# Moving the first loads of k, v and q into one GpSimd DMA row with the first weight matrix

## The chip, the cores and the metric

The kernel runs on one core of a Trainium2 chip. The metric is the device time of one execution in microseconds (us); the time of a run is about 1.8 us longer than the span of its trace. A single core has no second die to compare with, so I checked the granted TensorE clock of each run instead (the share of its full clock that TensorE was allowed): 0.99 to 1.0 in all but one kernel, which is told as such.

## The reference

For each of 8 batches and 8 heads (576 positions, head size 64) a linear attention: features of q and k are the positive part times a cosine and times a sine of the position, concatenated. Then one dense layer with a squared ReLU.

```python
k_p, q_p = phi(k), phi(q)                  # (B, H, S, 128)
kv  = einsum('bhsf,bhsd->bhfd', k_p, v);  z = k_p.sum(axis=2)
x   = einsum('bhsf,bhfd->bhsd', q_p, kv) / (einsum('bhsf,bhf->bhs', q_p, z) + 1e-6)
x   = x.transpose(0, 2, 1, 3).reshape(4608, 512)
out = maximum(x @ w_in, 0)**2 @ w_out      # w_in 512 x 2048, w_out 2048 x 512
```

## The kernel before

Positions of a batch are split in a main part (512, four blocks of 128) and a tail (64). `load` fetches one of q, k, v for a batch: one transfer of 1 MB (two halves for the first q), then two of 64 KB for the tail.

```python
def load(src, nm, b, eng, parts=1):
    main = inp.tile([P, H, J, D], F32, ...); tail = inp.tile([P, HH, D], F32, ...)
    for i in range(parts):
        eng.dma_start(out=main[:, :, js, :], in_=src[b, :, 0:MAIN, :]...)    # rows of 1 KB (512 B in halves)
    for g in range(2):
        eng.dma_start(out=tail[g*TAIL:(g+1)*TAIL], in_=src[b, ..., MAIN:S, :]...)   # rows of 256 B
```

`load_w1` fetches a quarter of w_in from the GpSimd queue and converts it to bf16 on the way (1 MB read, 512 KB written). The start of the program, which is all that the change touches:

```python
load_batch(0, nc.sync, "kv")
load(q, "q", 0, nc.sync, 2)
constants()                       # position constants, identity: GpSimd, ScalarE
warm(34)                          # filler products that keep TensorE running
for j in range(NS): att_k(0, j)   # features of k on VectorE (cos) and ScalarE (sin)
att_v(0, J - 1, nc.gpsimd, H - 1, H)   # GpSimd copies one head of v ...
att_v(0, 0, nc.vector); att_v(0, 1, nc.scalar); att_v(0, 2, nc.vector)
att_v(0, 3, nc.vector, 0, H - 1)       # ... VectorE the other seven of that block
att_v(0, J, nc.vector)                 # v's tail
for i in range(4): load_w1(i, 4)       # w_in, behind GpSimd's copy
load_batch(1, nc.gpsimd, "q"); load_w2(0, 4)   # [...] later loads, same queue
att_kv(0, 0); att_kv(0, 1)             # "kz": k features times v
att_feat(0, 0); att_feat(0, 1)         # features of q
# [...] transposes of q ("tq"), "num", division, transposes of x, then the w_in products ("hps")
```

The engines run their instructions in order (an experiment below shows VectorE held up for 2.21 us by this). Each DMA issue on GpSimd waits for the landing of the one eight issues back (in the profile of before the tenth issue, a tail of batch 1's k, waits 2.48 us, until the second quarter of w_in has landed). The w_in products of batch 0 come in eight groups; the first four each need a new quarter of w_in.

Of the kernel before, what the change touches and what calls it, by code (L numbers as in the profile page):

```python
# [19 lines left out]
def kernel(  # L20
# [9 lines left out]
    nc = tc.nc  # L30
    P = nc.NUM_PARTITIONS
    B, H, S, D = q.shape
# [6 lines left out]
    J = S // P  # L39
# [18 lines left out]

    kqv = {}

    def load(src, nm, b, eng, parts=1):
        main = inp.tile([P, H, J, D], F32, name=nm, tag=nm, bufs=2)
        tail = inp.tile([P, HH, D], F32, name=nm + "t", tag=nm + "t", bufs=2)
        for i in range(parts):
            js = slice(i * J // parts, (i + 1) * J // parts)
            eng.dma_start(
                out=main[:, :, js, :],
                in_=src[b, :, 0:MAIN, :].rearrange("h (p j) d -> p h j d", j=J)[:, :, js, :],
            )
        for g in range(2):  # L70
            eng.dma_start(
                out=tail[g * TAIL : (g + 1) * TAIL, :, :],
                in_=src[b, g * HH : (g + 1) * HH, MAIN:S, :].rearrange("h p d -> p h d"),
            )
        kqv[nm, b] = (main, tail)

    def load_batch(b, eng, order):
        for nm in order:
            load({"k": k, "v": v, "q": q}[nm], nm, b, eng)

    def piece(nm, b, j):
        main, tail = kqv[nm, b]
        return main[:, :, j, :] if j < J else tail[:, :, :]
# [8 lines left out]
    def constants():  # L92
        sidx = const.tile([P, J + 1], F32, name="sidx")
        for p0, p1, c, n, base, mult in [
            (0, P, 0, J, 0, J),
            (0, TAIL, J, 1, MAIN, 1),
            (TAIL, P, J, 1, MAIN, 1),
        ]:
            nc.gpsimd.iota(
                sidx[p0:p1, c : c + n],  # L100
                pattern=[[1, n]],
                base=base,
                channel_multiplier=mult,
                allow_small_or_imprecise_dtypes=True,
            )
        bias_pi2 = const.tile([P, 1], F32, name="bias_pi2")
        nc.vector.memset(bias_pi2, math.pi / 2.0)
        theta_scale = (math.pi / 2.0) / S
        nc.scalar.activation(cos_col, sidx, ACTF.Sin, bias=bias_pi2[:], scale=-theta_scale)
        nc.scalar.activation(sin_col, sidx, ACTF.Sin, bias=0.0, scale=theta_scale)  # L110
        make_identity(nc, ident)
# [5 lines left out]
    def load_w1(i, n):  # L117
        f0, f1 = i * DFF // n, (i + 1) * DFF // n
        nc.gpsimd.dma_start(  # L119
            out=w1sb[:, :, f0:f1],  # L120
            in_=moe_w_in[:, f0:f1].rearrange("(kb p) f -> p kb f", p=P),
        )

    def load_w2(i, n):
        h0, h1 = i * HB // n, (i + 1) * HB // n
        nc.gpsimd.dma_start(
            out=w2sb[:, h0:h1, :],
            in_=moe_w_out[h0 * P : h1 * P, :].rearrange("(hb p) f -> p hb f", p=P),
        )
# [62 lines left out]
    def att_k(b, j, cos=feat_cos):  # L192
        for f in (cos, feat_sin):
            f(kp_of(b, j), piece("k", b, j), j)

    def att_v(b, j, eng, h0=0, h1=H):
        copy = eng.copy if eng is nc.scalar else eng.tensor_copy
        vx, vxt = vexts[b % 2]
        if j == J:
            copy(out=vxt[:, :, 0:D], in_=piece("v", b, j))  # L200
        else:
            copy(out=vx[:, j, h0:h1, 0:D], in_=piece("v", b, j)[:, h0:h1, :])  # L202

    def warm(n):

        wm = ps_h.tile([P, 2, FP], F32, name="wm", tag="hps", bufs=2)
        for i in range(n):
            nc.tensor.matmul(
                out=wm[:, i % 2, :], lhsT=zeros[:, 0:P], rhs=zeros[:, :], start=True, stop=True
            )  # L210
# [13 lines left out]
    def att_kv(b, part):  # L224
        vx, vxt = vexts[b % 2]
        if part == 0:
            kvzs[b] = att.tile([P, H, E1], BF16, name="kvz", tag="kvz", bufs=2)
            kzs[b] = ps_a.tile([P, 2, FP], F32, name="kz", tag="pa", bufs=1)
        kz = kzs[b]




        for j in (0, 1) if part == 0 else range(2, NS):
            for hh in range(HH):
                for half in range(2):
                    h = half * HH + hh
                    if j < J:
                        lhsT, rhs = kp_of(b, j)[:, h, :], vx[:, j, h, :]
                    else:  # L240
                        p0, p1 = half * TAIL, (half + 1) * TAIL
                        lhsT, rhs = kp_of(b, j)[p0:p1, hh, :], vxt[p0:p1, hh, :]
                    nc.tensor.matmul(  # L243
                        out=kz[:, half, hh * E1 : (hh + 1) * E1],
                        lhsT=lhsT,
                        rhs=rhs,
                        start=(j == 0 and hh == 0),
                        stop=(j == J and hh == HH - 1),
                    )
        if part == 1 and b:  # L250
            att_kvz(b, nc.scalar.copy)

    def att_kvz(b, copy):
        copy(
            out=kvzs[b].rearrange("p (a h) e -> p a (h e)", a=2),
            in_=kzs[b][:, :, 0 : HH * E1],
        )

    def att_feat(b, j, parts="cs"):
        for c in parts:  # L260
            f = feat_cos if c == "c" else feat_sin
            f(qp_of(b, j), piece("q", b, j), j)
# [15 lines left out]
    def att_qT_pe(b, j, apart=False):  # L278

        nh = H if j < J else HH  # L280
        tq = ps_y.tile([P, H, P], BF16, name="tq", tag="yps", bufs=2)
        tqs[b, j] = [tq[:, 0:HH, :]]
        if apart:
            hi = ps_h.tile([P, HH, P], BF16, name="tqh", tag="hps", bufs=2)
            tqs[b, j].append(hi)
        elif nh == H:
            tqs[b, j].append(tq[:, HH:H, :])
        for h in range(nh):
            nc.tensor.transpose(  # L289
                tqs[b, j][h // HH][:, h % HH, :], qp_of(b, j)[:, h, :], ident[:, :]  # L290
            )

    def att_qT_copy(b, j, both=False):
        qpTs[b, j] = []
        for i, tq in enumerate(tqs[b, j]):
            t = att.tile([P, HH, P], BF16, name=f"qpTp{i}", tag=f"qpTp{i}", bufs=3)
            copy = nc.scalar.copy if both and i else nc.vector.tensor_copy
            copy(out=t[:, :, :], in_=tq[:, :, :])
            qpTs[b, j].append(t)
# [363 lines left out]
    for j in (2, 3):  # L663
# [12 lines left out]
        k=(8, 8, 8, 9, 9),  # L676
        f=(4, 5, 6, 12, 13),
        v=(10, 10, 10, 10, 10),
        kv=(11, 11),
# [9 lines left out]
        k=(21, 22, 23, 24, 25),  # L689
        f=(18, 19, 20, 22, 23),  # L690
        kv=(26, 26),
# [6 lines left out]
        k=(29, 31, 32, 34, 35),  # L698
        f=(27, 30, 33, 34, 34),
        kv=(36, 37),  # L700
# [3 lines left out]
    for b in range(4, B):  # L704
# [5 lines left out]
            k=(o, o, o + 1, o + 1, o + 2),  # L710
            f=(o + 4, o + 4, o + 5, o + 5, o + 6),
            kv=(o + 3, o + 4),
# [27 lines left out]
            fn2(*args)  # L740

    with tc.manual_schedule():
        load_batch(0, nc.sync, "kv")
        load(q, "q", 0, nc.sync, 2)
        constants()
        warm(34)
        for j in range(NS):
            att_k(0, j)
        att_v(0, J - 1, nc.gpsimd, H - 1, H)
        att_v(0, 0, nc.vector)  # L750
        att_v(0, 1, nc.scalar)
        att_v(0, 2, nc.vector)
        att_v(0, 3, nc.vector, 0, H - 1)
        att_v(0, J, nc.vector)
        for i in range(4):
            load_w1(i, 4)
        load_batch(1, nc.gpsimd, "q")
        load_w2(0, 4)
        load_batch(1, nc.gpsimd, "k")
        load_w2(1, 4)  # L760
        load_batch(1, nc.gpsimd, "v")
        for i in range(2, 4):
            load_w2(i, 4)
        load_batch(2, nc.gpsimd, "qkv")
        att_kv(0, 0)
        att_kv(0, 1)
        att_feat(0, 0)
        att_feat(0, 1)
        att_kvz(0, nc.vector.tensor_copy)
        warm(1)  # L770
        for j in range(2):
            att_qT_pe(0, j, True)
        for j in range(2):
            att_qT_copy(0, j, True)
            att_num(0, j, True)
        for j in range(2):
            att_div(0, j)
        att_feat(0, 2, "s")
        att_feat(0, 3, "s")
        for j in range(2):  # L780
            fill(4 - j)
            att_x_pe(0, j, True)
        att_feat(0, 2, "c")
        att_feat(0, 3, "c")
        for s in range(len(slots)):
            run(s)
# [29 lines left out]
```

## Time and profile before

| | before |
|---|---|
| time, first three runs | 289.8 us (289.28 to 289.86) |
| span of the profiled run, granted clock | 288.1 us, 1.000 |
| TensorE busy | 280.6 us, 97% |
| TensorE idle in the first 30 us | 3.13 us |
| k, v, first half of q landed at | 6.4, 11.1, 13.0 us |
| first and fourth group of w_in products start at | 17.98 and 26.09 us |

The rows of landings are read from the timelines: the time at which the first reader of a load starts after having waited for it. In a timeline the columns are start, duration, engine, line, operation, output and inputs, and in brackets the idle time before and its releaser. In a table of windows they are the stretch, its length, the busy time and number of instructions of TensorE, its weight loads, VectorE, ScalarE and GpSimd, then the granted clock, the busy share of the DMA engines and GB/s.

### The profile page before, as it was taken

To read this page: it belongs to the slowest core of one execution; us is meant where nothing else is said; L and a number is where in the kernel's file an instruction comes from. 1 tells how busy PE (TensorE), PEld (TensorE's weight loads), DVE (VectorE), ACT (ScalarE), POOL (GpSimd) and SP (SyncE) were. 2 spreads that over 40 slices of the span, in tenths; PEclk is the share of its full clock that TensorE was granted. 3 is DMA by queue.
4 is the path that set the end of the run, shared out by engine and by line. 5 is a ranking of instruction groups with operands and counts; after the bars stand their busy time and mean duration, and the time that the engine had idled before them with its cause. 6 is when DMAs were issued, how large, how long until landed. Compare 5 with 4: busy or idle time off the path is not lost.

```text
span 288.1 us, 7340 instructions
## 1 busy us (share of the span) xinstructions
PE 280.6 (97%) x3070; PEld 236.0 (82%) x3070; DVE 204.5 (71%) x457; ACT 161.8 (56%) x245; POOL 39.0 (14%) x67
## 2 busy tenths in 40 slices
PE   8899999999999999999999999999999999999995
PEld 3478845888678888898988888988998988889884
DVE  1576674588699399787598776977677877547485
ACT  3574753479759759455782348835695551155210
POOL 1462505650000000100002000000000000000002
PEclk9999999999999999999999999999999999999999
DMA  7999996999948799899619985399718820300015
GB/s 207 290 204 288 303 271 186 356 354 232 182 67 236 156 287 228 217 283 223 168 75 203 332 190 164 105 242 308 195 39 209 142 46 3 123 24 2 0 75 146
DMA packets 77825, 53.04 MB, mean 184 GB/s; under 512 B 52032, under 2 KB 73024, under 8 KB 77792
## 3 DMA queue, kind: packets, MB, share of 16 engines
q1 hardware_dynamic: 68000, 29.24, 43.6%
q0 software_dynamic: 9648, 23.20, 27.9%
q8 instruction: 24, 0.39, 0.6%
q10 hardware_dynamic: 144, 0.13, 0.1%
q14 instruction: 9, 0.07, 0.1%
HBM read 36.70 MB, written 9.44 MB: 160 GB/s over the span
## 4 chain that ended last, share of the span: by engine, by line
PE 85%; DMA 7%; DVE 2%; ACT 2%; issue 1%; POOL 1%; SPq 1%; ACTq 0%
PE hps L388 40%; PE ya L530 9%; PE yc L530 9%; PE yu L530 7%; PE yv L530 5%; DMA w1sb<-in_moe_w_in_dram 4%; PE num L315 3%; DMA v<-in_v_dram 3%; PE kz L243 3%; PE yps L461 2%; PE yps L437 2%; PE yh L437 2%; DVE ysb L542 1%; POOL w1sb L119 1%; PE tq L289 1%
## 5 line engine op out<-in xcount | busy, mean ns | idle before, releaser
L388 PEld LDWEIGHTS <-w1sb 128*128 128x128 bf16 x1344 | 113.4, 98 | 13.5 <-issue 2.0
L388 PE MATMUL hps<-xT,w1sb 128*128 128x256 bf16 (+1 forms) x1088 | 119.3, 266 | 1.4 <-DMA w1sb<-in_moe_w_in_dram 0.6
L396 ACT ACTIVATE rt<-hps 128x1024 bf16<-128x1024 f32 x72 | 73.6, 1023 | 68.4 <-PE hps L388 47.0
L403 DVE TENSOR_TENSOR gT<-rt 128x1024 bf16<-128x1024 bf16 x64 | 44.0, 687 | 20.0 <-ACT rt L396 20.0
L530 PEld LDWEIGHTS <-gs 128*128 128x128 bf16 x480 | 46.8, 98 | 5.4
L530 PEld LDWEIGHTS <-gT 128*128 128x128 bf16 x312 | 29.8, 98 | 3.4
L415 POOL DMA_DIRECT2D out_dram<-ysb x14 | 7.6, 541 | 170.7 <-DVE ysb L542 145.0
L183 ACT ACTIVATE kp<-k,sin_col 128x512 bf16<-128x512 f32 x32 | 22.4, 717 | 3.2 <-DMA k<-in_k_dram 3.2
L329 DVE TENSOR_TENSOR x<-num,rden 128x512 bf16<-128x512 f32 x32 | 22.1, 691 | 1.1
L183 ACT ACTIVATE qp<-q,sin_col 128x512 bf16<-128x512 f32 x32 | 22.0, 720 | 1.3 <-DMA q<-in_q_dram 1.3
L325 DVE TENSOR_SCALAR den<-num 128x8 f32<-128x8 f32 (+1 forms) x40 | 6.6, 164 | 21.2 <-PE num L315 21.0
L526 DVE TENSOR_TENSOR gs<-gT 128x1024 bf16<-128x1024 bf16 x26 | 17.8, 684 | 0.0
L173 DVE TENSOR_SCALAR qp<-q,cos_col 128x512 bf16<-128x512 f32 x32 | 15.9, 524 | 0.4 <-DMA q<-in_q_dram 0.4
L530 PE MATMUL ya<-w2t,gs 128*128 128x256 bf16 x120 | 15.6, 273 | 0.0
L530 PE MATMUL yu<-w2t,gs 128*128 128x256 bf16 x120 | 15.6, 273 | 0.0
L530 PE MATMUL yc<-w2sb,gs 128*128 128x256 bf16 x120 | 15.6, 273 | 0.0
L388 PE MATMUL hps<-xTt,w1sb 128*128 128x128 bf16 x256 | 15.1, 219 | 0.2 <-ACT rt L396 0.2
L202 ACT CAST vext<-v 128x512 bf16<-128x512 f32 x23 | 14.1, 614 | 1.7 <-DMA v<-in_v_dram 1.7
L530 PE MATMUL yu<-w2sb,gs 128*128 128x256 bf16 x112 | 14.5, 273 | 0.0
L581 ACT COPY s<-yu 128x256 f32<-128x256 f32 x14 | 5.2, 372 | 15.3 <-PE yu L530 15.3
L530 PE MATMUL yc<-w2sb,gT 128*128 128x256 bf16 x104 | 13.5, 273 | 0.0
L530 PE MATMUL yv<-w2t,gT 128*128 128x256 bf16 x104 | 13.5, 273 | 0.0
(99 smaller groups left out, 331.7 us busy)
## 6 DMA issues: line engine op xcount, KB each, us to landing
out_dram<-ysb POOLq DMA_DIRECT2D x14, 512.0 KB, 4.1
k<-in_k_dram SPq DMA_DIRECT2D x5, 1024.0 KB, 8.1
v<-in_v_dram SPq DMA_DIRECT2D x5, 1024.0 KB, 8.7
q<-in_q_dram SPq DMA_DIRECT2D x4, 1024.0 KB, 6.5
q<-in_q_dram POOLq DMA_DIRECT2D x3, 1024.0 KB, 12.4
k<-in_k_dram POOLq DMA_DIRECT2D x3, 1024.0 KB, 10.5
v<-in_v_dram POOLq DMA_DIRECT2D x3, 1024.0 KB, 9.3
w1sb<-in_moe_w_in_dram POOLq DMA_DIRECT2D x4, 512.0 KB, 9.4
```

Source lines behind the costliest of these rows:

```text
L173: nc.vector.tensor_scalar(out=dst[:, :, 0:D], in0=src, scalar1=0.0, scalar2=cos_col[:, j : j + 1], op0=ALU.max, op1=ALU.mult,)
L183: nc.scalar.activation(out=dst[:, :, D:F], in_=src, func=ACTF.Relu, scale=sin_col[:, j : j + 1])
L202: copy(out=vx[:, j, h0:h1, 0:D], in_=piece("v", b, j)[:, h0:h1, :])
L243: nc.tensor.matmul(out=kz[:, half, hh * E1 : (hh + 1) * E1], lhsT=lhsT, rhs=rhs, start=(j == 0 and hh == 0), stop=(j == J and hh == HH - 1),)
L315: nc.tensor.matmul(out=out, lhsT=lhsT, rhs=kvz[:, half * HH + hh, :], start=True, stop=True)
L329: nc.vector.tensor_tensor(out=x_of(b, j).rearrange("p (b k) (l d) -> p b k l d", b=n, l=2), in0=n4[:, :, :, 0:D].rearrange("p b (k l) d -> ...
L388: nc.tensor.matmul(out=out, lhsT=w1sb[:, kb, hb * P : (hb + 1) * P], rhs=rhs, start=(kb == 0), stop=(kb == KB - 1),)
L396: nc.scalar.activation(out=rt[:, :, :], in_=hps[:, :, :], func=ACTF.Relu)
L403: nc.vector.tensor_tensor(out=dst, in0=rt[:, :, :], in1=rt[:, :, :], op=ALU.mult)
L437: nc.tensor.matmul(out=ypss[b][tt], lhsT=gTs[b][:, hb, tt * P : (tt + 1) * P], rhs=w2sb[:, hb, :], start=(hb == 0), stop=(hb == HB - 1),)
L526: nc.vector.tensor_tensor(out=t[:, :, :], in0=in0, in1=in1, op=op)
L530: nc.tensor.matmul(out=acc, lhsT=lhs[:, hb, :], rhs=rhs[:, hb, :], start=(hb == 0), stop=(hb == HB2 - 1),)
```

## The change

The intent is that GpSimd no longer stands waiting for v before it may issue w_in, and that k, v, q and w_in follow each other in one row, that is one behind the other on GpSimd's DMA queue, without a gap.

```diff
-    def load(src, nm, b, eng, parts=1):
+    def load(src, nm, b, eng, parts=1, tail_eng=None):
...
         for g in range(2):
-            eng.dma_start(
+            (tail_eng or eng).dma_start(
...
-        load_batch(0, nc.sync, "kv")
-        load(q, "q", 0, nc.sync, 2)
+        load(k, "k", 0, nc.gpsimd, 1, nc.sync)
         constants()
+        load(v, "v", 0, nc.gpsimd, 1, nc.sync)
+        load(q, "q", 0, nc.gpsimd, 2, nc.sync)
         warm(34)
...
-        att_v(0, J - 1, nc.gpsimd, H - 1, H)
         att_v(0, 0, nc.vector)
         att_v(0, 1, nc.scalar)
         att_v(0, 2, nc.vector)
-        att_v(0, 3, nc.vector, 0, H - 1)
+        att_v(0, 3, nc.vector)
```

## The prediction

> **What bounds the kernel now.** I read the page first, then the busy times by stage over the whole span, then the chain that ended last, the TensorE and ScalarE/VectorE timelines of the first 29 us, and last the DMA in half-microsecond windows. The page's first line and the stage table say how little there is to win.
>
> ```profile
> PE 280.6 (97%) x3070; PEld 236.0 (82%) x3070; DVE 204.5 (71%) x457; ACT 161.8 (56%) x245; POOL 39.0 (14%) x67
> ```
>
> ```profile
> 0.00:30.00 30.00, 26.87 (x276) 18.17 (x277) 15.93 (x43) 15.23 (x23) 11.54 (x23) 1.00 1.04 246
> 30.00:60.00 30.00, 29.80 (x302) 20.64 (x300) 18.66 (x45) 16.03 (x25) 13.31 (x20) 1.00 0.98 288
> 60.00:120.00 60.00, 59.59 (x713) 50.08 (x711) 49.36 (x116) 46.68 (x75) 5.04 (x9) 1.00 0.89 210
> ```
>
> In the stage table the second figure after the stretch is the busy time of TensorE. From 30 us on TensorE is never idle for long (0.20 of 30 us, 0.41 of 60 us). So whatever the change does, it does before about 28 us; a start that is earlier by some amount moves the end by that amount, and nothing after 30 us gives more. In the head TensorE is idle 3.13 us, and its 35 filler products (9.96 us for the first 34) count as busy though they only keep it running until v arrives.
>
> The chain that ended last starts with the loads, not with arithmetic:
>
> ```profile
> 2.67 8.44 DMA v<-in_v_dram
> 11.11 0.05 issue
> 11.16 0.49 POOL vext L202
> 11.65 2.56 POOL w1sb L119 x3
> 14.22 11.82 DMA w1sb<-in_moe_w_in_dram
> 26.04 0.05 issue
> 26.09 1.92 PE hps L388 x16
> ```
>
> GpSimd waits for v (landed at 11.11 us), copies one head of it, and only then issues w_in. The fourth quarter of w_in lands at 26.04 us and the fourth w_in product starts at 26.09. That is the wait the change attacks. But the TensorE timeline shows how much of that wait is really empty:
>
> ```profile
> 13.79 0.40 PE L289 MATMUL tq<-ident,qp 128*128 128x128 bf16 x4 [0.49 <-ACT qp L183]
> ...
> 17.98 1.95 PE L388 MATMUL hps<-xT,w1sb 128*128 128x128 bf16 x32
> 19.77 1.06 PE L289 MATMUL tq<-ident,qp 128*128 128x128 bf16 x16
> 21.02 1.92 PE L388 MATMUL hps<-xT,w1sb 128*128 128x256 bf16 x16 [0.20 <-DMA w1sb<-in_moe_w_in_dram]
> 22.78 0.41 PE L315 MATMUL num<-kvz,qpTp 128*128 128x65 bf16 x8
> 23.55 1.92 PE L388 MATMUL hps<-xT,w1sb 128*128 128x256 bf16 x16 [0.36 <-DMA w1sb<-in_moe_w_in_dram]
> ```
>
> The bracket is the idle time before a group and what ended it. TensorE waits 0.20, 0.36 and (25.94 to 26.09) 0.15 us for the second, third and fourth quarters: 0.7 us together. The first quarter costs nothing. The start of that product (17.98) hangs on the other chain: q lands at 13.01 (ScalarE's first feature of q starts then, after 1.26 us of idleness), and 0.78 us later the transposes start; 4.97 us lie between q's landing and the first w_in product.
>
> The DMA in half-microsecond windows (last two figures: busy share of the 16 engines, GB/s written) shows the hole that the late issue makes:
>
> ```profile
> 12.50:13.00 0.50, 0.50 (x18) 0.39 (x14) 0.10 (x1) 0.00 (x0) 0.50 (x2) 1.00 1.00 264
> 13.00:13.50 0.50, 0.30 (x1) 0.00 (x1) 0.49 (x2) 0.49 (x1) 0.50 (x2) 1.00 0.98 181
> 13.50:14.00 0.50, 0.21 (x4) 0.21 (x5) 0.50 (x3) 0.50 (x2) 0.50 (x1) 1.00 0.33 65
> 14.00:14.50 0.50, 0.50 (x10) 0.34 (x8) 0.50 (x2) 0.40 (x2) 0.50 (x2) 1.00 0.96 139
> ```
>
> w_in was issued from 11.59, but its bytes flow only from about 14.0, some 2.3 us later, when the loads of q have run dry. So the hole is about 0.7 us, not 2.5: the DMA engines were busy with q meanwhile.
>
> **What the Trainium skill says.** "DMA: Bandwidth & Descriptors", section "Issuing engines are not separate DMA queues": all queues run on the same 16 engines, so moving a load between queues buys no bandwidth. The trace agrees: the share of the engines is 0.86 or more from 3 to 13.5 us with one queue and 1.15 or more from 14.5 to 24 us with the other. Same page, section "Latency and other measured facts": first byte after about 600 ns for the SyncE path and about 1 us for the GpSimd path. The trace has both, longer but in the same order: k issued at 0.74 flows from about 2.0 us (1.3 us), w_in issued at 11.59 from about 14.0 (2.3 us, nearer 1.4 after the end of its 0.95 us issue). Same page, section "Queues, rings and completion order": each engine takes turns between queues packet by packet. So the tails on SyncE will run beside k, while k, v, q and w_in on one queue follow each other. "SBUF — State Buffer", section "SBUF: two separate sides", warns that VectorE in a two-port mode can keep GpSimd from writing descriptors. In the trace the issues from 11.59 to 14.95, beside VectorE's copies of v, still took 0.75 to 0.95 us each, so I expect nothing from it here.
>
> **The change part by part.**
>
> 1. w_in no longer waits for v. Issues on GpSimd: k, then the constants (0.9 us of work), v, two halves of q, four of w_in; at 0.9 us each all are issued by about 9 us. w_in's bytes then follow q's without the hole. When? k, v and q with tails are 3.54 MB. Before, they were written by about 13.5 us. The new first bytes of k come about 1 us later than before (2.3 against 1.3 us after issue), but the SyncE tails fill that gap partly: six issues of about 0.65 us carry 64 KB each, some 100 GB/s from 2 us on. Rate afterwards: k ran at about 370 GB/s from SyncE (4.0 to 5.5 us: 381, 379, 361), v and q at about 333; on the GpSimd queue the q of batch 1, same 1 KB rows, ran at 404 GB/s (24.5 to 27 us). I take 375 for k and v and 340 for q's 512 B pieces. From about 3 us: k with the remaining tails 1.35 MB, 3.7 us, 6.7; v 1.05 MB, 2.7 us, 9.4; q's halves 0.52 MB each, 1.5 us each, 10.9 and 12.4. w_in starts at 12.4 instead of 14.0: 1.6 us earlier. Each quarter takes 2.55 us (14.0 to 24.2 for four), and lands about 1.8 us after its bytes are on average through (24.2 against 26.04). So quarters two to four land at about 19.3, 21.8 and 24.4, against 21.0, 23.5 and 26.04.
>
> 2. q and v. Landing comes after the average byte, because the slowest engine decides: 1.4 us for v and 1.7 for q's first half before; 1.8 to 2.2 on the GpSimd queue (w_in, and q of batch 1: through at about 27, landed at 29.1). So v lands at about 11.1 (as before), q's first half at about 12.7 instead of 13.0: 0.3 us earlier, and I would not be surprised by 0.5 either way.
>
> 3. k lands later, about 7.3 to 7.5 against 6.44, because of the late start and of all six tails beside it. ScalarE's k work takes 2.95 us (6.44 to 9.39) and is followed by 1.74 us of idleness before v; VectorE's takes 1.95 with 2.74 idle. Both slacks swallow 1 us. Cost 0.
>
> 4. v's copy: VectorE's piece grows from 448 to 512 columns, 414 to 464 ns at most (those are the shortest and longest of that line), so +0.05 us; GpSimd's 0.49 us vanish, which lay beside VectorE's 1.5 us. VectorE had 0.41 us of slack before q. Cost 0 to 0.05.
>
> 5. The order of instructions on TensorE and ScalarE is unchanged apart from buffer names (the comparison of the two programs shows this). GpSimd gains four loads; each of its DMA issues waits for the landing of the one eight places back, and as four were added in front of all, batch 1's k still waits for w_in's first quarter. No new throttle.
>
> Sum: the first w_in product at 17.98 - 0.3 = 17.7. Without waits for w_in the second starts when the transposes are done (20.83 - 0.3 = 20.5, landed 19.3), the third 2.17 us later (22.7, landed 21.8), the fourth 2.39 us after that (25.1, landed 24.4). Against 26.09 that is 1.0 us: 0.7 from w_in, 0.3 from q. The 1.6 us by which w_in itself comes earlier are more than can be used. 289.8 - 1.0 = 288.8 us.
>
> **Rivals.** (a) v or q becomes the new wait: if the GpSimd queue runs these loads at 330 rather than 375, q's first half lands at about 13.3 and the first w_in product comes 0.3 late; then 0.7 - 0.3, a gain of 0.4 us, 289.4. For it: HWDGE's v and q ran at 333, the tails are 256 B pieces, and the first GpSimd load may start even later. Against: 404 GB/s measured on that queue. (b) Everything comes earlier: if lag and rate are both good, q lands at 12.0 and the gain is 1.7 us (288.1); more is barred by the 34 filler products, which hold TensorE until 11.15, so the transposes, 1.7 us of kz and filler later (11.61 to 13.30), can't start before about 12.9 against 13.79: at most 0.9 from q, 1.6 in all. (c) The chain's face value: 26.04 was set by v's wait, so w_in's 1.6 us or more pass to the end. Against it stand the gaps of only 0.7 us. (d) A loss: v lands so late (12 us or more) that kz and VectorE's work slide behind it and TensorE stands idle after its filler; each us of v beyond about 11.5 costs the same, perhaps 0.5 us net, 290.3.
>
> **Range and chances.** The gain is 0.7 (sure, if w_in leads q's chain) plus q's shift of 0.3 with a spread of about 0.5, and the runs of before differ by 0.6 us. So 288.8, with 288.0 to 289.8 holding 8 in 10. 2% is 5.8 us, nearly twice all the idle time of TensorE in the head: faster 0.01, same 0.98, slower 0.01.
>
> **What would show each step right or wrong.** Right: no hole near 13.5 us in the DMA windows and w_in's plateau of about 200 GB/s beginning near 12.4; the w_in products carry no wait on a w_in DMA; the first of them at about 17.7 and the fourth at about 25.1; k's features start near 7.4; v's copies near 11.1; ScalarE's q feature near 12.7; the chain's head goes through q, not w_in. Wrong: the products still wait for w_in (then w_in came less than about 1 us earlier), or v lands after 11.6 with TensorE idle before kz (then the GpSimd queue is slow for these loads), or TensorE shows new idle time after 30 us.

## The result, and the profile after

The changed kernel took 289.08 us (median of 4 runs, 288.72 to 289.87) beside 289.73 us of the kernel before (289.28 to 289.86). The ratio was 0.9984, with a 95% interval from 0.996 to 1.0008. A ratio here is the mean time of one kernel's fast runs over that of the other's of the same rounds, so not quite the ratio of the medians. The measured time lies in the predicted range; the forecast gain of 1.0 us does not show clearly.

The profiled run of the changed kernel was its slowest (289.87 us, span 288.1 us, as long as that of before). The page's first line and the first two rows of the stage table of the changed kernel:

```profile
PE 278.9 (97%) x3064; PEld 235.9 (82%) x3070; DVE 204.0 (71%) x457; ACT 161.7 (56%) x245; POOL 42.5 (15%) x70
```

```profile
0.00:30.00 30.00, 25.71 (x277) 18.14 (x279) 16.20 (x43) 15.39 (x24) 15.09 (x27) 1.00 1.01 255
30.00:60.00 30.00, 29.64 (x299) 20.75 (x300) 18.25 (x46) 16.11 (x25) 14.07 (x20) 1.00 0.96 287
```

TensorE is now idle 4.29 us of the first 30, more than before (3.13), but not all of this is time lost: the same 34 filler products took 9.10 us here and 9.96 before (8.82 to 9.34 and 9.96 to 10.41 in the three profiles of each), and what makes them shorter was not looked into. The chain that ended last no longer waits for v to land, but passes through GpSimd's issues and then w_in:

```profile
3.51 0.94 POOL v L66
4.45 1.75 POOL q L66 x2
6.21 2.20 POOL w1sb L119 x3
8.41 17.41 DMA w1sb<-in_moe_w_in_dram
25.82 0.05 issue
25.87 1.92 PE hps L388 x16
```

w_in is issued from 6.2 us on instead of 11.6, and yet its last quarter lands only 0.2 us earlier, at 25.82. (In two later profiles of the changed kernel this chain runs through the landing of q and of v instead, not of w_in.) In TensorE's timeline the waits have changed places:

```profile
12.55 1.13 PE L243 MATMUL kz<-vext,kp 128*128 128x65 bf16 x32 [2.26 <-DVE vext L202]
...
14.31 0.40 PE L289 MATMUL tq<-ident,qp 128*128 128x128 bf16 x4 [0.40 <-ACT qp L183]
...
18.51 1.95 PE L388 MATMUL hps<-xT,w1sb 128*128 128x128 bf16 x32
```

TensorE stands 2.26 us for v, which lands at 12.07 us; q lands at 13.54, and the first w_in group starts at 18.51, 0.53 us later than in the profile of before. In return the second and third groups no longer wait for w_in (they start at 21.19 and 23.31), and the fourth waits 0.17 us. The DMA hole at 13.5 us is gone, in the same half-microsecond windows:

```profile
13.00:13.50 0.50, 0.50 (x23) 0.50 (x19) 0.41 (x2) 0.00 (x0) 0.00 (x0) 1.00 1.07 344
13.50:14.00 0.50, 0.41 (x14) 0.33 (x11) 0.46 (x2) 0.46 (x1) 0.20 (x1) 1.00 1.14 239
```

Where the time went stands in two longer windows and the DMA's count by queue. First the kernel before, from 2 to 4.5 and from 4.5 to 13 us:

```profile
2.00:4.50 2.50, 2.50 (x7) 0.91 (x6) 0.00 (x0) 1.23 (x3) 0.00 (x0) 1.00 0.90 274
4.50:13.00 8.50, 8.03 (x68) 4.04 (x66) 3.41 (x9) 3.58 (x6) 1.84 (x3) 1.00 1.06 321
```

Then the changed kernel, and three half-microseconds of it:

```profile
2.00:4.50 2.50, 2.50 (x7) 0.91 (x6) 0.00 (x0) 1.23 (x3) 2.18 (x8) 1.00 0.56 117
4.50:13.00 8.50, 6.24 (x42) 2.99 (x41) 3.29 (x8) 3.58 (x6) 6.55 (x8) 1.00 1.02 355
```

```profile
3.50:4.00 0.50, 0.50 (x3) 0.15 (x1) 0.00 (x0) 0.00 (x0) 0.49 (x1) 1.00 0.88 124
4.00:4.50 0.50, 0.50 (x2) 0.15 (x1) 0.00 (x0) 0.00 (x0) 0.50 (x2) 1.00 0.48 173
4.50:5.00 0.50, 0.50 (x4) 0.24 (x3) 0.00 (x0) 0.00 (x0) 0.50 (x1) 1.00 1.12 399
```

The last figure is GB/s. Up to 4.5 us the changed kernel wrote 0.29 MB (2.5 us at 117 GB/s), before 0.69 MB: k's late start costs 0.39 MB. From 4.5 to 13 us it wrote 3.02 MB against 2.73 and won 0.29 MB back. The count by queue for 4.5 to 13 us (packets, MB, share of the engines) shows a reason for the better rate. First before, then after:

```profile
q1 hardware_dynamic: 4696, 2.72, 106.1%
```

```profile
q0 software_dynamic: 725, 2.78, 89.8%
q1 hardware_dynamic: 981, 0.24, 12.6%
```

q1 is the SyncE queue and q0 that of GpSimd. SyncE moved 2.72 MB in 4696 packets, 0.6 KB each; GpSimd moved 2.78 MB in 725 packets of 3.8 KB. That larger packets are the cause of the rate goes with these counts, but was not tested by itself.

### The profile page after: what moved, and what is told of

The parts are those of the page before. It is cut to its first block, busy times and chain, and to the rows that moved or that the text cites. A ratio compares the mean times of both kernels' runs of the same rounds, so it can differ in the third digit from the quotient of the medians.

```text
span 288.1 us, 7331 instructions
## 1 busy us (share of the span) xinstructions
PE 278.9 (97%) x3064; PEld 235.9 (82%) x3070; DVE 204.0 (71%) x457; ACT 161.7 (56%) x245; POOL 42.5 (15%) x70
## 3 DMA queue, kind: packets, MB, share of 16 engines
q1 hardware_dynamic: 63840, 26.09, 40.4%
## 4 chain that ended last, share of the span: by engine, by line
PE 85%; DMA 6%; POOL 2%; DVE 2%; ACT 2%; issue 1%; POOLq 0%; ACTq 0%
PE hps L388 40%; PE ya L530 9%; PE yc L530 9%; PE yu L530 7%; DMA w1sb<-in_moe_w_in_dram 6%; PE yv L530 5%; PE num L315 3%; PE kz L243 3%; PE yps L461 2%; PE yps L437 2%; PE yh L437 2%; DVE ysb L542 1%; PE tq L289 1%; POOL w1sb L119 1%; DVE u L542 1%
## 5 line engine op out<-in xcount | busy, mean ns | idle before, releaser
L173 DVE TENSOR_SCALAR qp<-q,cos_col 128x512 bf16<-128x512 f32 x32 | 15.0, 496 | 0.1
L173 DVE TENSOR_SCALAR kp<-k,cos_col 128x512 bf16<-128x512 f32 x21 | 10.0, 501 | 7.1 <-DMA k<-in_k_dram 7.1
L530 PE MATMUL yc<-w2sb,gT 128*128 128x256 bf16 x104 | 13.5, 273 | 0.0
```

The lines of the kernel that those rows point to most:

```text
L173: nc.vector.tensor_scalar(out=dst[:, :, 0:D], in0=src, scalar1=0.0, scalar2=cos_col[:, j : j + 1], op0=ALU.max, op1=ALU.mult,)
L530: nc.tensor.matmul(out=acc, lhsT=lhs[:, hb, :], rhs=rhs[:, hb, :], start=(hb == 0), stop=(hb == HB2 - 1),)
```

## The experiments

**The changed kernel twice more, and the kernel before twice more.** No edit. First the yardstick of the first set of runs:

> The changed kernel once more, unaltered, because its first four runs left the interval from -0.4% to +0.1%. Theory A (the first load on the GpSimd queue starts its bytes about 2 us late, and this gives back most of what the filled hole and the faster queue win): between 0.1 and 0.3% faster than before, some 289.1 us, the fourth w_in product at about 25.9 us. Rival R0 (the difference was chance): ratio 1.000 within 0.1%.

It took 289.05 us (6 runs, 288.91 to 289.58) beside 289.33 us of before (11 runs): ratio 0.9994, interval 0.9978 to 1.0011. And in the second set of runs:

> The changed kernel unaltered, a third time, on the chip of these runs and as their yardstick. The fourth w_in product started at 25.87 us in one profile and 24.93 in another, so the loads at the start vary by about 1 us from run to run. Expected 289.0 us, 0.1 to 0.2% under the kernel before, and the whole span = start of the fourth w_in product + 262.2 us within 0.1 us, as in every profile so far of the new arrangement.

It took 289.06 us (288.45 to 289.55) beside 289.34 us (11 runs, 288.5 to 290.42): ratio 0.9984, interval 0.9963 to 1.0006. Over all three sets the 16 runs of the changed kernel have a mean of 289.12 us and the 26 of before 289.40. The difference is 0.28 us, with a standard error of 0.14 us worked out from the two spreads (0.40 and 0.50 us). So neither theory A nor chance is beaten by one set alone; together they speak for a small gain. Theory A's 25.9 us for the fourth w_in product did not come true in this profile (24.93, in the table below). Two more profiles of the kernel before, one run each, so their state is unknown, at clocks of 0.998 and 0.999:

> The kernel before, unaltered, for a second profile. Its 15 runs beside the changed kernel's 16 spread from 288.5 to 290.4 us, so its only profile (289.9 us in that run, span 288.1) may be one of its slow ones. If the loads at the start make the spread: the fourth w_in product starts between 24.9 and 26.1 us, and span = that start + 262.0 us within 0.1. If something later makes it: the start stays at 26.1 while the span changes.

> The same once more: a third profile of the kernel before, with the same two readings.

| profile | k landed | v | q, first half | first w_in group | fourth group | span |
|---|---|---|---|---|---|---|
| before | 6.44 | 11.13 | 13.01 | 17.98 | 26.09 | 288.1 |
| before, second | 6.11 | 10.90 | 12.69 | 17.66 | 25.62 | 287.6 |
| before, third | 6.45 | 10.86 | 12.63 | 17.60 | 25.48 | 287.4 |
| changed | 8.50 | 12.07 | 13.54 | 18.51 | 25.87 | 288.1 |
| changed, second | 8.27 | 11.66 | 13.08 | 18.05 | 24.93 | 287.1 |
| changed, third | 7.52 | 11.31 | 12.70 | 17.66 | 24.61 | 286.8 |

The span is the start of the fourth group plus 261.9 to 262.0 us before, and plus 262.2 in the changed kernel. So all variation from run to run in these six profiles comes from the loads at the start. The one profile that I predicted from was the slowest of the three of before in all but k. In the third profile of before the waits for w_in are still there:

```profile
22.93 1.92 PE L388 MATMUL hps<-xT,w1sb 128*128 128x256 bf16 x16 [0.34 <-DMA w1sb<-in_moe_w_in_dram]
...
25.48 1.92 PE L388 MATMUL hps<-xT,w1sb 128*128 128x256 bf16 x16 [0.17 <-DMA w1sb<-in_moe_w_in_dram]
```

In the third profile of the changed kernel the same groups start without one:

```profile
22.33 1.91 PE L388 MATMUL hps<-xT,w1sb 128*128 128x256 bf16 x16
...
24.61 1.92 PE L388 MATMUL hps<-xT,w1sb 128*128 128x256 bf16 x16
```

**One part alone: GpSimd copies nothing, the loads stay where they were.**

```diff
 # on the kernel before
-        att_v(0, J - 1, nc.gpsimd, H - 1, H)
 ...
-        att_v(0, 3, nc.vector, 0, H - 1)
+        att_v(0, 3, nc.vector)
```

> The kernel before with one part of the change alone: GpSimd copies no head of v, so w_in is issued from about 2 us, while k, v and q stay on the SyncE queue. Theory A (all loads share the same engines, so what counts is the order of the bytes, and the row is what keeps w_in behind q): w_in's 4 MB run beside k, v and q; k lands at 8 us or later, q's first half between 17 and 20 us, the first w_in product at 22 to 25, the fourth at 29 to 32, and the kernel takes 293 to 296 us. Rival C (taking GpSimd's wait for v away is the whole gain and the queue does not matter): like the changed kernel or better, 288.5 to 289.1 us.

It took 311.5 us (4 runs), ratio 1.0778 (1.0743 to 1.0814). Rival C is out: without the row, the early w_in ruins the start. The direction of theory A held, but its size was far off, and k landed at 6.48 us, not after 8. q's first half landed at 28.55 us and its second at 37.06, because not w_in alone but all that GpSimd had issued behind it took turns with q. The count from 15 to 25 us:

```profile
q0 software_dynamic: 1334, 2.12, 87.6%
q1 hardware_dynamic: 1336, 0.56, 28.2%
```

The engines took 1334 packets from GpSimd and 1336 from SyncE: turn by turn, as the prediction had it. But the turns are packets and not bytes, so the queue with the large packets got 2.12 MB written and the other 0.56. In the same time the granted clock of TensorE, which had been busy for 0.34 us of the 5 before, fell to half (the last but two column):

```profile
10.00:15.00 5.00, 0.34 (x2) 0.06 (x1) 0.00 (x0) 0.00 (x0) 0.90 (x1) 0.98 1.17 247
15.00:20.00 5.00, 1.92 (x32) 1.85 (x32) 1.10 (x3) 0.62 (x1) 0.99 (x2) 0.50 1.21 205
```

This kernel's mean clock was 0.96, part of its loss, and the reason why its 311.5 us are not to be read as DMA time alone. The loss lies in the start: the fourth w_in group began at 47.29 us, and from there to the end it took 261.9 us, as before.

**The wait for v put back into the changed kernel.**

```diff
 # on the changed kernel, ahead of w_in's issue
+        att_v(0, J - 1, nc.gpsimd, H - 1, H)
 ...
-        att_v(0, 3, nc.vector)
+        att_v(0, 3, nc.vector, 0, H - 1)
```

> The changed kernel with GpSimd's copy of one head of v put back ahead of w_in's issue (VectorE copies seven heads again). If the wait for v is worth something only as a hole in the DMA: v lands at 12.1, w_in is issued at 12.6, its bytes flow from about 14.9 instead of 13.6, fourth quarter near 27.1 us, 290.2 us. Rival (the DMA of w_in is hidden behind q's chain in any case): same as the changed kernel, 289.1 us.

It took 290.2 us, as expected; ratio to before 1.0027 (1.0011 to 1.0042), and its mean is 0.9 us above that of the changed kernel in the same rounds. v landed at 11.57, w_in was issued at 12.04, and the hole is back, wider than in the kernel before:

```profile
13.50:14.00 0.50, 0.27 (x9) 0.27 (x11) 0.50 (x2) 0.50 (x2) 0.50 (x2) 1.00 0.83 66
14.00:14.50 0.50, 0.50 (x8) 0.38 (x8) 0.50 (x2) 0.29 (x1) 0.50 (x2) 1.00 0.77 63
```

The third and fourth groups waited 0.34 and 0.15 us for w_in, the fourth started at 26.19 (its quarter came some 0.9 us earlier than I had written). So inside the new arrangement, taking GpSimd's wait away is worth 0.9 us: that part of the prediction's mechanism is shown.

**k back on SyncE.**

```diff
 # on the changed kernel
-        load(k, "k", 0, nc.gpsimd, 1, nc.sync)
+        load(k, "k", 0, nc.sync)
```

> The changed kernel with k alone back on the SyncE queue; v, q and w_in stay in one row on GpSimd. Theory A: from 2.0 to 4.5 us the DMA writes about 0.68 MB as in the kernel before, not 0.29 MB, so the row is some 0.39 MB or 1.0 us ahead: v lands near 11.0, q's first half near 12.5, the first w_in product near 17.5 and the fourth near 24.8 us; 288.1 us, 0.3% under the changed kernel. Rival B (the GpSimd queue's rate, not its start, decides): k on the slower queue costs as much as it wins, 289.1 us or more. A miss of A would be k landing after 9 us because v's packets take the engines from it.

It took 289.95 us, ratio 1.0027 (1.0007 to 1.0047): slower, against theory A's total, although the loads behaved better than A said. From 2 to 4.5 us the DMA wrote 261 GB/s (0.65 MB); k landed at 6.36, v at 10.27 and q at 11.72 us, each about 1 us or more ahead of every profile of the changed kernel. But the first w_in group started at 18.77. The trace names the wait:

```profile
13.62 0.30 DVE L200 CAST vextt<-vt 128x256 bf16<-128x256 f32 x1 [2.21 <-DMA vt<-in_v_dram]
13.83 1.00 DVE L173 TENSOR_SCALAR qp<-q,cos_col 128x512 bf16<-128x512 f32 x2
```

v's tail, issued on SyncE at 2.67 and 3.3 us, was there only at 13.62, and VectorE, which works in order, could not start q's features before. From 9 to 13 us the SyncE queue again got as many turns as GpSimd (451 and 450 packets), but only 0.11 MB against 1.22. Rival B's number came out (289 or more), but not by its cause.

**All tails in the row.**

```diff
 # on the changed kernel
-        load(k, "k", 0, nc.gpsimd, 1, nc.sync)
+        load(k, "k", 0, nc.gpsimd)          # v and q likewise
```

> The changed kernel with the six tail loads also on the GpSimd queue, each pair behind its main load, so nothing runs on SyncE at the start. Theory A: the DMA engines stand idle until k's bytes flow at about 4.3 us, 0.29 MB of tails no longer fits in that time, and all behind k comes about 0.7 us later: q's first half near 14.0, the fourth w_in quarter near 26.5 us; 289.7 us. Rival T (the tails' 256 B pieces beside k are what makes k late): k lands at 7.8 us or earlier and v at 11.5 or earlier, 288.6 us.

It took 289.28 us, ratio 0.9996 (0.9979 to 1.0012), between the two and as fast as the changed kernel within the spread. Theory A had q's first half near 14.0; it landed at 12.68, k at 7.64 and v at 11.09. Rival T's landings for k and v came true. That k comes earlier without small tails beside it is not shown, as the changed kernel had k at 7.52 in its third profile; v came 0.2 us ahead of the earliest of its three. Rival T's time did not (288.6 expected): six more issues on GpSimd delayed those of w_in, the first to 10.12 us and the other three to 11.36 and after, and the third group waited 0.43 us for w_in. Up to 13 us this kernel wrote 3.30 MB (93 GB/s for 2.5 us and 361 for 8.5), the three profiles of the changed kernel 3.31, 3.46 and 3.48. So the 0.29 MB that theory A had missing were not missing: at most 0.18 were. With nothing on SyncE this run also shows the start of the GpSimd queue by itself: no bytes before 3.0 us, then 164, 82 and 221 GB/s in half-microseconds, and 401 from 4.5 on. The slow start is thus not made by the tails beside k.

**v's tail in the row, k on SyncE.** What the last two runs point to: start early on SyncE with k, and send through the row whatever v's and q's readers need.

```diff
 # on the kernel with k on SyncE
-        load(v, "v", 0, nc.gpsimd, 1, nc.sync)
+        load(v, "v", 0, nc.gpsimd)
```

> k and its tail and q's tail on SyncE; v, v's tail, q and w_in in the GpSimd row. In the run with k on SyncE, v and q came about 1.4 us earlier but VectorE then stood for v's tail until 13.62 us, because the tail's small packets on SyncE had to share with the row's. If that starved tail is what spoiled it: v lands near 10.3, its tail before 11, q's first half near 12.0, first w_in product near 17.0, fourth between 24.2 and 24.7 us; 288.2 to 288.6 us, 0.3% under the kernel before and 0.2% under the changed one. If not (k's place on SyncE costs by itself): 289 us or more.

It took 288.4 us (288.33 to 288.8), ratio 0.9966 (0.9947 to 0.9985), as expected. k landed at 6.27, v at 10.56, q at 12.51; the first w_in group started at 17.47 (0.5 us later than I had said) and the fourth at 24.35 (in the range given). The same tail moved from one queue to the other is thus worth 1.5 us between these two kernels, which shows that the starved tail spoiled the run before.

**q's tail behind w_in.**

```diff
 # on the kernel above; q's tail leaves SyncE (its old issue is taken out by an argument of load)
 ...
         for i in range(4): load_w1(i, 4)
+        load_tail(q, "q", 0, nc.gpsimd)
```

> As the kernel with v's tail in the row, and q's tail, which nothing needs before the thirteenth w_in product, moved behind w_in in the row. It takes 0.13 MB out of the way of w_in, about 0.35 us at 385 GB/s: fourth w_in product 0.2 to 0.3 us earlier than there if w_in still sets it; 288.0 to 288.4 us. If by then q's chain sets it, no difference.

It took 288.02 us (6 runs, 287.35 to 288.27) beside 289.34 us of before: ratio 0.9948 (0.9928 to 0.9967), the best version found. Its mean (287.95 us) is 1.1 us below that of the changed kernel in the same rounds (289.02). The TensorE timeline of its profiled run:

```profile
10.62 1.27 PE L248 MATMUL kz<-vext,kp 128*128 128x65 bf16 x32 [0.30 <-DVE vext L207]
...
16.64 1.95 PE L393 MATMUL hps<-xT,w1sb 128*128 128x128 bf16 x32
...
23.67 1.92 PE L393 MATMUL hps<-xT,w1sb 128*128 128x256 bf16 x16
```

v landed at 10.14 and q at 11.68, and the w_in groups start 0.7 to 0.8 us earlier than in the kernel above. That is more than the 0.2 to 0.3 us expected; this profile was the fastest of its six runs, and the medians differ by 0.4 us. v and q came earlier too, by 0.42 and 0.83 us, so the gain did not come only from w_in's shorter way, as expected; with one profile of each kernel the two can't be told apart.

## Why the prediction was right or wrong

The predicted time, range and class hold. The size of the gain, 1.0 us, was about three and a half times the pooled 0.28. Of the prediction's own signs of being wrong one came true: v landed after 11.6 us in two of the three profiles of the changed kernel (12.07, 11.66), with TensorE idle for 2.26 and 2.13 us before kz. In its own terms, with the means of the three profiles of each kernel:

1. **w_in no longer waits for v: right, and worth more than said.** From the first to the fourth w_in group the kernel before took 8.11, 7.96 and 7.88 us, the changed one 7.36, 6.88 and 6.95: 0.92 us less, where the sum had 0.7. The prediction kept the spacing of 2.17 and 2.39 us between later groups from the old timeline; without the waits it is 1.99 and 2.21 (second profile: 20.73, 22.72, 24.93).
2. **The term that failed: "From about 3 us: k with the remaining tails 1.35 MB, 3.7 us, 6.7".** The first packets of the GpSimd queue did come at about 3 us, but the full rate did not. The issue of k began at 1.28 us and not at 0.74, took 1.05 us, and between 2 and 4.5 us only 0.29 to 0.36 MB were written, where 0.1 MB to 3 us and 375 GB/s from there would give 0.66. The missing 0.3 MB are 0.9 us at the 355 to 367 GB/s that followed. So k landed at 7.5 to 8.5 instead of 7.3 to 7.5. The old profile had the slow start in it, and the prediction read over it: w_in's bytes did not flow "only from about 14.0", its first 10 packets came between 13.0 and 13.5 us, then 6, 50 and 100 in the half-microseconds that followed. The changed kernel's k came with 8, 13, 19 and 48 from 3.0 us on. So part of the hole at 13.5 was this queue's slow start, and the same was to be expected of k. Why the queue starts slowly stays open. (The 3.7 us, and 2.7 for v, are 3.6 and 2.8 at the prediction's own 375 GB/s; the slips cancel.)
3. **q: 0.3 us earlier predicted, 0.33 later measured** (mean 13.11 against 12.78). This follows from point 2 (with k back on SyncE q landed at 11.72), and it moves the first w_in group from 17.75 to 18.07 on average. v came at 11.3 to 12.1 where 11.1 stood. Rival (a) named the outcome (a gain of 0.4, with q's first half about 0.3 us late), but put it down to a slow rate, with a later start only as a remark in its favour; the rate was good (355 to 367 GB/s against 321 to 323 before), and the late start ate it. Rival (b)'s bar fell: the filler did not hold TensorE until 11.15 (kz started at 10.62 in the best version), and q's chain could give more than 0.9 us (the first w_in group started there at 16.64, 1.34 earlier than in the profile predicted from).
4. **k's lateness and v's copy cost nothing: right, for k in part by luck.** In the profiled run ScalarE ended k's features at 11.46 and waited 0.61 us for v. The slack of 1.74 us had shrunk to that, and it was left only because v was late too: had v landed at 11.1, as predicted, k's features would have held up ScalarE for 0.4 us.
5. **VectorE beside GpSimd: "I expect nothing" held for GpSimd's issues, but not the other way round.** The issues of w_in and the next q, in part beside VectorE's features, took 0.75 to 1.10 us each, where they had taken 0.75 to 0.95. But VectorE's four cosine features of k took 1.67 us before and 2.11, 2.45 and 2.82 in the three profiles of the changed kernel, while GpSimd was issuing. With the copy put back, GpSimd issued nothing in that time, and they took 1.68; in the five other experiments, where GpSimd issued loads early, they took 1.93 to 2.19. It cost nothing that the profiles show, and what makes it was not tested.
6. **An unforeseen 0.25 us at the end.** From the start of the last VectorE addition to the end of the span the kernel before took 3.2 to 3.3 us and the changed one 3.5, in all three profiles of each; the best version took 3.2 again. What does it stays open.

The sum of the measured parts is -0.92 + 0.32 + 0.25 = -0.35 us, which agrees with the pooled -0.28. The prediction's start of the fourth w_in group, 25.1 us, is met by the mean of the three profiles, 25.14, but by luck: the first group came 0.37 us later than its 17.7, and the stretch from there to the fourth was 0.34 shorter than its 7.4. The gain fell short for two other reasons: the profile of before came from a slow run (its fourth group at 26.09, mean of three 25.73: 0.36 us), and point 6 took 0.25. The stated range also held the case of no gain, so that the time lies in it says little. What makes the loads vary by up to 1.3 us from run to run was not settled.

## What to carry to other kernels

Before moving a load to another queue, work out what the DMA engines do in every microsecond of the start: a wait that looks like 12 us in the chain can be a hole of 0.7 us in the DMA. Start the first load on the queue that starts fastest, keep what follows in the row whose order you control, and do not leave a small load that someone needs soon on another queue beside a stream of large packets without counting its turns: here it cost 1.5 us. And take more than one profile before trusting a sub-microsecond sum.

## What the Trainium skill lacked or had wrong

- "DMA: Bandwidth & Descriptors", "Issuing engines are not separate DMA queues", says that several issuing engines only save issue time. Here the queue also changed the packets (0.6 KB on SyncE, 3.8 KB on GpSimd in the loads of k, v and q), who is served (0.56 against 2.12 MB in 10 us at equal packet counts) and, with the cause not tested, the rate (321 to 323 GB/s before, 355 to 367 after). The page does have the turns by packet and a preferred upper size of a GpSimd packet; it lacks the size of SyncE's packets and what the difference does.
- Same page, "Latency and other measured facts": first byte after about 0.6 and 1 us. Measured from the start of the issue, k's bytes flowed after 1.3 us on SyncE; on GpSimd its first packets came 1.7 us after its issue had begun and the full rate only after more than 3 us (4.5 us in the trace). The page has no figure for this slow start.
- "SBUF — State Buffer", "SBUF: two separate sides", warns of GpSimd's descriptor writing being held up by VectorE, and says in general that either of the two can block the other. It has no figure for loads that slow VectorE: here its features of k took 2.11 to 2.82 us instead of 1.67 while GpSimd issued loads. That this is the blocking the page means is not shown.
- No page that I read tells how much the loads at the start of a program vary: the same kernel had its fourth w_in group between 24.61 and 25.87 us in three profiles.
